# One reader for the third product's bank, and an expert's six scaled additions spread over the next products, in a three-stage attention and mixture-of-experts kernel

## The chip, the cores and the metric

The kernel runs on one core of a Trainium2 chip. The metric is the device time of one execution in microseconds (us): before the change the median of three runs is 1606.64 us (1606.39 to 1607.98). One further execution was recorded by the hardware profiler; its rows are what this document reads.

The engines are called by the profile's names: PE is TensorE's matmul side, PEld its weight load, DVE is VectorE, ACT is ScalarE, POOL is GpSimd, and SP issues the DMAs.

## The reference

Three layers follow each other, on 1536 tokens of width 512, all in float32:

```
attn_out = _attn_ref(q, k, v, proj)         # attention inside hash buckets
x = _moe_ref(x=x, w_in, w_out)              # g = h * tanh(softplus(h)); 512 -> 2048 -> 512
P = exp(x @ w_gate - max); 8 rounds of row and column normalisation
for e in range(8):
    h = np.maximum(x @ w1[e], 0.0)          # 512 -> 1024
    ye = h @ w2[e]                          # 1024 -> 512
    out += P[:, e:e + 1] * ye
```

The change lies in the last loop, for experts 1 to 7 (expert 0 is computed with the middle layer).

## The kernel before

**Precision.** Each float32 operand is split into a rounded high part and the rest; a product is three matmuls (high by high, high by rest, rest by high). So every value that is to be multiplied again needs two instructions: one that writes the rounded part, one that writes the rest.

**Units.** The loop at the end of the file runs over 56 units: two halves of the tokens (768 each), seven experts, four blocks of 256 hidden columns. A unit has two passes. In the first, seven block products (`PRODUCTS`, a Strassen-like scheme with seven products in place of eight) give the four blocks of the hidden matrix, called 11, 22, 21 and 12, each 128 partitions by 384 tokens. In the second (`second`, `second_mm`), 36 matmuls multiply the four blocks, after the ReLU, by a slice of `w2` and add into six PSUM tiles `y`, one for each 128 tokens of the half. The `y` tiles collect over the four units of an expert. Then `gather` (L1199) adds each of the six, scaled by its column of `P`, to the result in `acc`.

**Banks.** The seven products share two PSUM banks, bank 0 and bank 1. A product is six matmuls (L1122, two blocks of the contraction by three parts). Products 0, 2, 4 and 6 go to bank 0, products 1, 3 and 5 to bank 1. Product 4 starts bank 0 anew; products 2, 3, 5 and 6 add to what their bank holds. After each product, `post` reads the bank: after product 0 ACT copies it to `p1` (L1149); after 1, 3, 4, 5 and 6 DVE adds something to it (L1142: `u`, `v`, and the blocks 22, 21 and 12). After product 2 the bank holds block 11 and is read twice: ACT writes its ReLU, rounded (`rounded`, L1130), and DVE copies it (L1155), since L1135 needs the unrounded block later for the rest. A product that writes a bank waits until the bank has been read.

**Order.** Every engine's order is the order of the program text (the scheduler is manual). Each unit also prepares the weights of later units: ACT rounds them (L982, L983, L1000, L1007), POOL forms sums and rests (L987, L988, L994 to L997, L1004, L1011), SP loads the next block after two of these. After every fourth unit the six `gather`s stand in DVE's order directly behind the second pass, before the next unit's `u`:

```
    def settle():
        for d in done:
            gather(*d)
        done.clear()
```

In the last unit, `settle` comes after each matmul instead, so that a tile is added as soon as it is complete.

Of the kernel before, what the change touches and what calls it, by code (L numbers as in the profile page):

```python
# [57 lines left out]
def lsh_attention_moe_kernel(  # L58
# [13 lines left out]
    nc = tc.nc  # L72
# [974 lines left out]
    for i in range(RING_A + NX + 1, NW):  # L1047
        need = free[i - RING] + 1 if i >= RING else 0
        if NATT <= i < N64:
            nd = max(nd, free_dec.get(i - NDEC, 0))  # L1050
            for j in range(2):
                d = int(nd)
# [11 lines left out]
    for n in range(NST + LAG):  # L1064
# [30 lines left out]
        s=wb_p.tile([P, 2, 1024], F32R, name="ws"), a=wb_p.tile([P, 2, 768], F32R, name="wa"),  # L1095
# [17 lines left out]
    bank, val, hid_u, y_t = {}, {}, {}, {}  # L1113

    def product(u, s):
        a, b, x, first = PRODUCTS[s]
        if first:
            bank[x] = ps_u.tile([P, 512], F32, tag=f"u{(u + x) % 2}", name="u")[:, :HALF]
        n = 0
        for kc in range(KC // 2):  # L1120
            for m, mm in ((0, 0), (0, 1), (1, 0)):
                nc.tensor.matmul(bank[x], weight(u, a, m, kc), moving(u, b, mm, kc), start=(first and n == 0), stop=(n == 5), skip_group_check=not first)  # L1122
                n += 1

    def temp(tag, bufs=1):
        return c_p.tile([P, HALF], F32, tag=tag, name=tag, bufs=bufs)

    def rounded(u, c, src):
        hi = h_p.tile([P, HALF], F32R, tag=f"h{c}", name="gh")
        nc.scalar.activation(hi, src, AF.Relu)  # L1130
        hid_u[u, c] = [hi]

    def rest(u, c, src):
        lo = h_p.tile([P, HALF], F32R, tag=f"l{c}", name="gl")
        nc.vector.scalar_tensor_tensor(  # L1135
            out=lo, in0=src, scalar=0.0, in1=f32(hid_u[u, c][0]), op0=ALU.max, op1=ALU.subtract
        )
        hid_u[u, c].append(lo)

    def total(tag, x, y):  # L1140
        t = val[tag] = temp(tag)
        nc.vector.tensor_add(t, x, y)  # L1142
        return t

    def post(u, s):
        a, b = bank[0], bank.get(1)
        if s == 0:
            val["p1"] = temp("p1")
            nc.scalar.copy(val["p1"], a)  # L1149
        elif s == 1:  # L1150
            total("u", b, val["p1"])
        elif s == 2:
            rounded(u, "11", a)
            val["c11"] = temp("c11")
            nc.vector.tensor_copy(val["c11"], a)  # L1155
        elif s == 3:
            total("v", b, val["p1"])
        elif s == 4:
            rounded(u, "22", total("c22", a, val["v"]))
        elif s == 5:  # L1160
            rounded(u, "21", total("c21", b, val["p1"]))
        else:
            rounded(u, "12", total("c12", a, val["u"]))
            for c in ("11", "22", "21", "12"):
                rest(u, c, val["c" + c])

    def second(u):
        tiles = {c: range(3 * int(c[1]) - 3, 3 * int(c[1])) for c in ("11", "22", "21", "12")}
        order = [(c, t, m) for c in ("11", "22") for t in tiles[c] for m in (0, 1)]
        if u == NU - 1:  # L1170
            for c, d in (("11", "21"), ("22", "12")):
                for t in tiles[c]:
                    order += [(c, t, 2)] + [(d, t, m) for m in range(3)]
        else:
            order += [(c, t, 2) for c in ("11", "22") for t in tiles[c]]
            order += [(c, t, m) for c in ("21", "12") for t in tiles[c] for m in (0, 1)]
            order += [(c, t, 2) for c in ("21", "12") for t in tiles[c]]
        return [
            (c, t, m, all(x[1] != t for x in order[:n]), all(x[1] != t for x in order[n + 1:]))
            for n, (c, t, m) in enumerate(order)  # L1180
        ]

    def second_mm(u, c, t, m, first, last):
        g, e, k = unit(u)
        if first and k == 0:
            y_t[t] = ps_z.tile([P, 512], F32, tag=f"z{t}", name="y")
        hi, lo = hid_u[u, c]
        y = wbuf[u % 2]["w"][:, int(m == 1), (int(c[0]) - 1) * 512:int(c[0]) * 512]
        nc.tensor.matmul(  # L1189
            y_t[t], (hi, hi, lo)[m][:, t % 3 * P:(t % 3 + 1) * P], y,  # L1190
            start=(k == 0 and first), stop=(k == NF // 2 - 1 and last),
        )
        if last and k == NF // 2 - 1:
            done.append((g, e, t))

    def gather(g, e, t):
        i = g * 6 + t
        dst = acc[:, i // KC, i % KC, :]
        nc.vector.scalar_tensor_tensor(  # L1199
            out=dst, in0=y_t[t], scalar=prob[:, i, e:e + 1], in1=dst, op0=ALU.mult, op1=ALU.add  # L1200
        )
        if e == E - 1:
            nc.sync.dma_start(out=out[i * P:(i + 1) * P, :], in_=dst)
# [7 lines left out]
    NRUN = 4  # L1211
# [30 lines left out]

    done = []

    def settle():
        for d in done:
            gather(*d)
        done.clear()

    def run_jobs(u, s):  # L1250
        for f in jobs.pop((u, s), []):
            f()

    for u in range(NU):
        run_jobs(u, -1)
        for s in range(NP1):
            product(u, s)
            post(u, s)
            run_jobs(u, s)
        downs = second(u)  # L1260
        for r in range(NRUN):
            for x in downs[len(downs) * r // NRUN:len(downs) * (r + 1) // NRUN]:
                second_mm(u, *x)
                if u == NU - 1:
                    settle()
            settle()
            run_jobs(u, NP1 + r)
    assert not jobs, jobs.keys()

# [49 lines left out]
```

## Time and profile before

| | |
|---|---|
| median of three runs | 1606.64 us |
| the profiled execution | 1608.38 us |
| its span, first to last instruction | 1606.6 us |
| PE busy | 1560.1 us, 97% |
| PEld busy | 1335.7 us, 83% |
| DVE busy | 957.3 us, 60% |
| POOL busy | 875.9 us, 55% |
| ACT busy | 642.4 us, 40% |
| mean granted TensorE clock | 0.999 |

The loop over the 56 units fills the span from about 704 us to its end. How to read the rows: a group of the timeline starts at the time in the first column, lasts as long as the second says, and the brackets at its end give how long the engine had been idle before it and what ended that. "x6" is the number of instructions in the group. In a query for one line, the three durations are the shortest, the median and the longest.

### The profile page before, as it was taken

To read this page: it belongs to the slowest core of one execution; us is meant where nothing else is said; L and a number is where in the kernel's file an instruction comes from. 1 tells how busy PE (TensorE), PEld (TensorE's weight loads), DVE (VectorE), ACT (ScalarE), POOL (GpSimd) and SP (SyncE) were. 2 spreads that over 40 slices of the span, in tenths; PEclk is the share of its full clock that TensorE was granted. 3 is DMA by queue.
4 is the path that set the end of the run, shared out by engine and by line. 5 is a ranking of instruction groups with operands and counts; after the bars stand their busy time and mean duration, and the time that the engine had idled before them with its cause. 6 is when DMAs were issued, how large, how long until landed. Compare 5 with 4: busy or idle time off the path is not lost.

```text
span 1606.6 us, 20403 instructions
## 1 busy us (share of the span) xinstructions
PE 1560.1 (97%) x7407; PEld 1335.7 (83%) x7407; DVE 957.3 (60%) x1536; ACT 642.4 (40%) x1167; POOL 875.9 (55%) x697
## 2 busy tenths in 40 slices
PE   7889999999999999999999999999999999999998
PEld 5777777888888878888888888888888888888887
DVE  7999998687883223666553544767535444445353
ACT  4767766644333322233333333333433333333331
POOL 4787867443333330236666666666666666666661
PEclk9999999999999999999999999999999999999999
DMA  6645442021222010012222222222322222222211
GB/s 144 170 111 132 122 129 72 27 77 54 66 66 79 0 53 1 27 40 66 66 66 66 66 66 66 66 66 66 105 66 66 66 66 66 66 66 66 66 53 40
DMA packets 62644, 113.46 MB, mean 71 GB/s; under 512 B 18176, under 2 KB 18920, under 8 KB 62544
## 3 DMA queue, kind: packets, MB, share of 16 engines
q1 hardware_dynamic: 62544, 112.17, 23.6%
q8 instruction: 58, 0.95, 0.3%
q14 instruction: 42, 0.34, 0.1%
HBM read 89.22 MB, written 3.15 MB: 57 GB/s over the span
## 4 chain that ended last, share of the span: by engine, by line
PE 80%; DVE 14%; ACT 2%; DMA 2%; issue 1%; SPq 0%; POOL 0%; ACTq 0%; DVEq 0%
PE y L1189 27%; PE u L1122 21%; PE y L823 12%; PE h L787 4%; PE h L789 4%; PE h L788 4%; DVE acc L1199 3%; PE pav L487 3%; DVE mx L399 2%; DVE c L1155 2%; ACT gh L1130 1%; PE ps L385 1%; PE pst L437 1%; PE pst L438 1%; DVE bit L343 0%
## 5 line engine op out<-in xcount | busy, mean ns | idle before, releaser
L1142 DVE TENSOR_TENSOR u<-u,p 128x384 f32<-128x384 f32 x56 | 31.1, 555 | 251.6 <-PE u L1122 251.6
L449 POOL TENSOR_TENSOR plo<-p,ph 128x384 fp32r<-128x384 f32 x128 | 142.5, 1124 | 69.1 <-ACT ph L446 37.3
L1130 ACT ACTIVATE gh<-c 128x384 fp32r<-128x384 f32 x168 | 88.3, 525 | 209.3 <-DVE c L1142 209.3
L1135 DVE SCALAR_TENSOR_TENSOR gl<-c,gh 128x384 fp32r<-128x384 f32 x224 | 168.5, 814 | 0.0
L1189 PE MATMUL y<-ww,gh 128*128 128x512 f32 x672 | 163.4, 391 | 0.0
L1189 PE MATMUL y<-w,gh 128*128 128x512 f32 x672 | 162.6, 391 | 0.0
L1189 PEld LDWEIGHTS y<-w,gh 128*128 128x128 f32 x672 | 125.7, 188 | 25.2
L1189 PEld LDWEIGHTS y<-ww,gh 128*128 128x128 f32 x672 | 125.7, 188 | 25.2
L1011 POOL TENSOR_TENSOR w<-stage,w 128x1024 fp32r<-128x1024 f32 x28 | 66.9, 2391 | 83.0 <-ACT w L1007 83.0
L157 POOL TENSOR_TENSOR stage<-stage,sgn 128x512 f32<-128x512 f32 x32 | 46.5, 1453 | 119.9 <-DVE sgn L155 48.3
L823 PE MATMUL y<-gh,w 128*128 128x512 f32 x336 | 110.3, 389 | 0.0
L1004 POOL TENSOR_TENSOR w<-sraw,w 128x1024 fp32r<-128x1024 f32 x28 | 68.5, 2447 | 76.0 <-ACT w L1000 76.0
L443 ACT ACTIVATE p<-pst 128x384 f32<-128x384 f32 x192 | 93.1, 489 | 36.1 <-PE pst L438 30.7
L1011 POOL TENSOR_TENSOR ww<-stage,ww 128x1024 fp32r<-128x1024 f32 x28 | 67.1, 2395 | 72.8 <-ACT ww L1007 72.8
L787 PE MATMUL h<-xh,w 128*128 128x512 f32 x252 | 99.5, 395 | 0.0
L987 POOL TENSOR_TENSOR wa<-stage,wa 128x512 fp32r<-128x512 f32 x28 | 38.5, 1374 | 109.6 <-ACT wa L982 85.8
L399 DVE TENSOR_REDUCE mx<-ps 128x1 f32<-128x768 f32 x95 | 89.9, 946 | 13.9 <-PE ps L385 13.3
L788 PE MATMUL h<-xl,w 128*128 128x512 f32 x252 | 98.2, 390 | 0.0
L789 PE MATMUL h<-xh,w 128*128 128x512 f32 x252 | 98.1, 389 | 0.0
L1122 PE MATMUL u<-tw,w 128*128 128x384 f32 x420 | 85.8, 344 | 8.5 <-DVE u L1142 5.1
L1122 PE MATMUL u<-tw,ws 128*128 128x384 f32 x420 | 88.0, 344 | 4.6 <-DVE c L1155 4.6
L1122 PEld LDWEIGHTS u<-tw,w 128*128 128x128 f32 x420 | 72.5, 188 | 17.5 <-DVE u L1142 9.3
(246 smaller groups left out, 4006.6 us busy)
## 6 DMA issues: line engine op xcount, KB each, us to landing
stage<-in_w_dram SPq DMA_DIRECT2D x152, 512.0 KB
raw<-in_qk_dram SPq DMA_DIRECT2D x13, 384.0 KB
wx<-hi SPq DMA_DIRECT2D x20, 192.0 KB
vt<-in_v_dram SPq DMA_DIRECT2D x16, 192.0 KB
out_dram<-acc SPq DMA_DIRECT2D x12, 256.0 KB
zq<-hi SPq DMA_DIRECT2D x11, 192.0 KB
ak<-hi SPq DMA_DIRECT2D x11, 192.0 KB
zq<-lo SPq DMA_DIRECT2D x11, 192.0 KB
```

Source lines behind the costliest of these rows:

```text
L399: nc.vector.tensor_reduce(out=m[:, t:t + 1], in_=s_t[t][:, :, :HALF], axis=AX.XY, op=ALU.max)
L443: nc.scalar.activation(p_t[u, c], st_t.pop((u, c))[:, :HALF], AF.Exp, scale=0.125)
L449: (nc.gpsimd if e == "P" else nc.vector).tensor_sub(out, in0, in1)
L787: nc.tensor.matmul(t, wt[:, 0, f], xh[:, kc, c], start=(kc == 0), stop=False)
L788: nc.tensor.matmul(t, wt[:, 0, f], xl[:, kc, c], start=False, stop=False)
L789: nc.tensor.matmul(t, wt[:, 1, f], xh[:, kc, c], start=False, stop=(kc == KC - 1))
L823: nc.tensor.matmul(yps[j], x, y, start=(head and m == 0), stop=(tail and m == 2))
L1011: nc.gpsimd.tensor_sub(y[:, 1, :], t, f32(y)[:, 0, :])
L1122: nc.tensor.matmul(bank[x], weight(u, a, m, kc), moving(u, b, mm, kc), start=(first and n == 0), stop=(n == 5), skip_group_check=not first)
L1130: nc.scalar.activation(hi, src, AF.Relu)
L1135: nc.vector.scalar_tensor_tensor(out=lo, in0=src, scalar=0.0, in1=f32(hid_u[u, c][0]), op0=ALU.max, op1=ALU.subtract)
L1189: nc.tensor.matmul(y_t[t], (hi, hi, lo)[m][:, t % 3 * P:(t % 3 + 1) * P], y, start=(k == 0 and first), stop=(k == NF // 2 - 1 and last),)
```

## The change

After product 2, ACT copies the bank into `c11` and rounds from that copy; DVE's copy goes. `settle` takes a number: two of an expert's six additions stay behind the second pass, the other four are written after products 0, 2, 4 and 5 of the next unit.

```diff
         elif s == 2:
-            rounded(u, "11", a)
             val["c11"] = temp("c11")
-            nc.vector.tensor_copy(val["c11"], a)
+            nc.scalar.copy(val["c11"], a)
+            rounded(u, "11", val["c11"])
         elif s == 3:
...
-    def settle():
-        for d in done:
+    def settle(n=None):
+        for d in done[:n]:
             gather(*d)
-        done.clear()
+        del done[:n]
...
             product(u, s)
             post(u, s)
+            settle(s in (0, 2, 4, 5))
             run_jobs(u, s)
...
                 if u == NU - 1:
                     settle()
-            settle()
+            if r == NRUN - 1:
+                settle(2)
             run_jobs(u, NP1 + r)
```

ACT's order in a unit, from the weight rounding that begins it to the first three ReLUs (`p` is `p1`, `u` the bank, `c` the blocks):

```order
 L1007 CAST w_76<-stage 128x1024
 L1149 COPY p_6888<-u 128x384
-L1130 ACTIVATE gh<-u 128x384
+L1154 COPY c_6909<-u 128x384
+L1130 ACTIVATE gh<-c_6909 128x384
 L1130 ACTIVATE gh<-c_6928 128x384
 L1130 ACTIVATE gh<-c_6938 128x384
```

ACT has one instruction more, and the first one behind `p1` is now the copy; the ReLU reads SBUF.

DVE's order in the first unit of an expert, before, from the six additions on:

```order
L1199 SCALAR_TENSOR_TENSOR acc<-y,prob,acc 128x512 x6
L1142 TENSOR_TENSOR u<-u,p_7804 128x384
L1155 COPY c_7827<-u 128x384
L1142 TENSOR_TENSOR v<-u,p_7804 128x384
L1142 TENSOR_TENSOR c_7844<-u,v 128x384
L1142 TENSOR_TENSOR c_7854<-u,p_7804 128x384
L1142 TENSOR_TENSOR c_7864<-u 128x384
L1135 SCALAR_TENSOR_TENSOR gl<-c_7827,gh 128x384
```

And in the changed kernel, the same place:

```order
L1199 SCALAR_TENSOR_TENSOR acc<-y,prob,acc 128x512 x3
L1142 TENSOR_TENSOR u<-u,p_7800 128x384
L1199 SCALAR_TENSOR_TENSOR acc<-y,prob,acc 128x512
L1142 TENSOR_TENSOR v<-u,p_7800 128x384
L1142 TENSOR_TENSOR c_7842<-u,v 128x384
L1199 SCALAR_TENSOR_TENSOR acc<-y,prob,acc 128x512
L1142 TENSOR_TENSOR c_7853<-u,p_7800 128x384
L1199 SCALAR_TENSOR_TENSOR acc<-y,prob,acc 128x512
L1142 TENSOR_TENSOR c_7864<-u 128x384
L1135 SCALAR_TENSOR_TENSOR gl<-c_7822,gh 128x384
```

Three additions now stand before `u` (two behind the second pass, one after product 0), the fourth before `v`, the fifth between the blocks 22 and 21, the sixth between 21 and 12; the copy of the bank is gone. In the other units DVE's order is the same but for the missing copy.

## Rows read from the trace of the kernel before

**Rows 1.** The page: busy us (share of the span) x instructions of each engine.
```profile
PE 1560.1 (97%) x7407; PEld 1335.7 (83%) x7407; DVE 957.3 (60%) x1536; ACT 642.4 (40%) x1167; POOL 875.9 (55%) x697
```

**Rows 2.** Waits of PEld from 700 us on: total us, times, longest.
```profile
PEld u L1122 <- DVE c L1155: 21.9, 43, 1.4
PEld u L1122 <- DVE u L1142: 9.3, 13, 1.5
```

**Rows 3.** Timeline, an ordinary unit's products: start, us, engine, line, operation [idle before].
```profile
1251.85 0.48 ACT L1149 COPY p<-u 128x384 f32<-128x384 f32 x1
...
1252.91 0.56 DVE L1142 TENSOR_TENSOR u<-u,p 128x384 f32<-128x384 f32 x1 [6.84 <-PE u L1122]
...
1253.52 1.07 PEld L1122 LDWEIGHTS u<-tw,w 128*128 128x128 f32 x6
...
1253.93 0.49 ACT L1130 ACTIVATE gh<-u 128x384 fp32r<-128x384 f32 x1 [1.60 <-PE u L1122]
...
1254.45 0.56 DVE L1155 COPY c<-u 128x384 f32<-128x384 f32 x1 [0.99 <-ACT gh L1130]
1254.95 0.56 DVE L1142 TENSOR_TENSOR v<-u,p 128x384 f32<-128x384 f32 x1
...
1255.07 1.01 PEld L1122 LDWEIGHTS u<-tw,w 128*128 128x128 f32 x6 [0.48 <-DVE c L1155]
...
1256.06 1.06 PEld L1122 LDWEIGHTS u<-tw,wx 128*128 128x128 f32 x6
```

**Rows 4.** Timeline, the first unit of an expert.
```profile
1281.57 4.05 DVE L1199 SCALAR_TENSOR_TENSOR acc<-y,prob,acc 128x512 f32<-128x512 f32 x6 [3.54 <-PE y L1189]
...
1285.53 0.55 DVE L1142 TENSOR_TENSOR u<-u,p 128x384 f32<-128x384 f32 x1
...
1286.14 2.06 PEld L1122 LDWEIGHTS u<-tw,w 128*128 128x128 f32 x12 [0.64 <-DVE u L1142]
...
1287.51 0.56 DVE L1142 TENSOR_TENSOR v<-u,p 128x384 f32<-128x384 f32 x1 [0.53 <-PE u L1122]
...
1288.18 1.05 PEld L1122 LDWEIGHTS u<-tw,wx 128*128 128x128 f32 x6
...
1288.55 0.56 DVE L1142 TENSOR_TENSOR c<-u,v 128x384 f32<-128x384 f32 x1 [0.48 <-PE u L1122]
...
1289.59 0.56 DVE L1142 TENSOR_TENSOR c<-u,p 128x384 f32<-128x384 f32 x1 [0.48 <-PE u L1122]
...
1290.43 2.92 PE L1189 MATMUL y<-w,gh 128*128 128x512 f32 x12
1290.63 0.56 DVE L1142 TENSOR_TENSOR c<-u 128x384 f32<-128x384 f32 x1 [0.48 <-PE u L1122]
1291.11 3.06 DVE L1135 SCALAR_TENSOR_TENSOR gl<-c,gh 128x384 fp32r<-128x384 f32 x4
...
1292.40 1.35 POOL L987 TENSOR_TENSOR wx<-stage,wx 128x512 fp32r<-128x512 f32 x1 [3.26 <-ACT wx L982]
```

**Rows 5.** Timeline, the very first unit, and PEld in the first unit after four.
```profile
708.63 0.48 ACT L1130 ACTIVATE gh<-u 128x384 fp32r<-128x384 f32 x1
...
709.76 1.00 PEld L1122 LDWEIGHTS u<-tw,w 128*128 128x128 f32 x6 [1.45 <-DVE c L1155]
...
773.66 2.06 PEld L1122 LDWEIGHTS u<-tw,w 128*128 128x128 f32 x12 [1.53 <-DVE u L1142]
```

**Rows 6.** Queries by line: duration ns min/median/max, first and last start.
```profile
L1149 ACT COPY p<-u x56: 481/481/483, 705.5 to 1588.1; 128x384 f32<-128x384 f32 x56
...
L1155 DVE COPY c<-u x56: 542/558/559, 709.2 to 1590.7; 128x384 f32<-128x384 f32 x56
...
L1135 DVE SCALAR_TENSOR_TENSOR gl<-c,gh x224: 546/552/1657, 713.7 to 1596.6; 128x384 fp32r<-128x384 f32 x112
```

**Rows 7.** One unit's stretch: us, busy (x) by engine, PEclk, DMA share, GB/s.
```profile
1256.00:1272.00 16.00, 15.84 (x80) 14.07 (x79) 6.25 (x10) 5.37 (x9) 9.93 (x9) 1.00 0.20 66
```

**Rows 8.** Line L1007 on ACT: its engine sat idle before it (us, times) until.
```profile
  PE y L1189: 278.5, 54
```

## The prediction

> **What bounds the kernel now.** The first view is the page's busy table: PE is busy for 97% of the span [rows 1], so only its idle time and what delays its matmuls can be won. A share of 97% hides small stalls, because a matmul that waits overlaps the one before it; the weight loads in front of the matmuls (PEld, 83%) show them better. So the second view is the list of waits of PEld, from the start of the 56 units on. It has two rows and no others: 43 waits for DVE's copy in L1155, 21.9 us, and 13 for DVE's `u` in L1142, 9.3 us [rows 2]. 43 + 13 = 56: one stall in each unit, 31.2 us in all.
>
> The third view is the timeline, for the place of each. In an ordinary unit ACT's ReLU of block 11 reads bank 0 at 1253.93, DVE's copy of the same bank starts at 1254.45, behind it, and ends at 1255.01; product 4, which writes bank 0 anew, starts its loads at 1255.07 after 0.48 us idle [rows 3]. In the first unit of an expert the six additions hold DVE from 1281.57 to 1285.62, `u` ends at 1286.08, and product 3, which adds to the bank that `u` reads, starts at 1286.14 after 0.64 us idle [rows 4]. The stall there is earlier, so that product 4 finds its bank free.
>
> That an idle stretch of PEld is lost time is seen by comparing starts. From product 3 to product 5 it is 1256.06 - 1253.52 = 2.54 us where product 4 stalls [rows 3], and 1288.18 - 1286.14 = 2.04 us where it doesn't [rows 4]: 0.50 against the 0.48 shown. One product is thus 1.02 us. PE's granted clock in such a stretch is 1.00, its upper level (2.4 GHz), with the stalls in it [rows 7].
>
> **The copy.** What goes is one DVE copy per unit (0.558 us, L1155 [rows 6]) and the wait of product 4 for it. What comes is one ACT copy per unit; the nearest row is ACT's copy of the same shape from the same kind of bank, L1149, 0.481 us [rows 6]. From product 3's first load at time 0 the times in an ordinary unit are [rows 3, 4, 6]:
> - ACT starts at 1253.93 - 1253.52 = 0.41, as its ReLU did. The copy ends at 0.41 + 0.48 = 0.89. From the reader's end to PE's load the rows show 0.06 (1255.01 to 1255.07; 1286.08 to 1286.14), so the bank is free at 0.95. Product 4 is due at 1.02. It doesn't wait, with 0.07 to spare. The upper bound for the copy's duration is the DVE copy, 0.558: free at 1.03, a stall of 0.01. The lower is 0.48, no stall. I take 0.48, the same operation on the same engine.
> - `v` is next. It reads bank 1 after product 3, and product 5 waits for it. In the first unit of an expert, where DVE had nothing before it, it started 1287.51 - 1286.14 = 1.37 after product 3's first load, so it ends at 1.93, free at 1.99; product 5 is due at 2.04. No wait, 0.05 to spare. Should `v` start only at 1254.95 - 1253.52 = 1.43, where it does now behind the copy, it would be free at 2.05, a stall of 0.01.
> - Block 22 (product 4 to product 6) has the same distance as `v` and didn't stall in either unit.
>
> The other edge of the step: the ReLU now stands behind the copy on ACT and reads SBUF. Nothing on ACT is due before block 22's ReLU, a product later, and the rounded block 11 is needed by the second pass, more than 2 us later. ACT is busy for 5.37 of 16 us [rows 7], and 0.5 us more is hidden in that idle time. DVE's rest of block 11 (L1135) needs `c11` only after block 12. So the stall of an ordinary unit goes, with nothing in its place.
>
> The very first unit is an exception: its stall is 1.45 us, since ACT had other roundings before its ReLU at 708.63 [rows 5]. The copy there ends at 708.63 + 0.48 = 709.11, PE may go at 709.17 instead of 709.76: 0.59 won, 0.86 kept.
>
> **The additions.** An addition takes 4.05 / 6 = 0.68 us in sequence [rows 4]. Two stay behind the second pass, the third follows after product 0, and they begin at 1281.57 as before and end near 1283.6. `u` can't begin before product 1 ends; PE reaches product 3's load at 1286.14 - 0.64 = 1285.50 if it isn't held, and in the ordinary unit `u` starts 1253.52 - 1252.91 = 0.61 before that load. So `u` is free to start at 1284.89, over 1 us after the third addition, and the 0.64 us go. Of the unit after the first expert, 1.53 us [rows 5], the 0.89 us above the others is the scaling (L903) that stands between its additions and `u`; it fits into that 1 us too.
>
> The fourth addition stands between `u` and `v`: from 1285.45 to 1286.13, and `v` is due at 1285.50 + 1.37 = 1286.87. The fifth stands between block 22, which ends at 1288.55 - 0.64 + 0.56 = 1288.47, and block 21, due at 1289.59 - 0.64 = 1288.95. It ends at 1289.15, so block 21 is 0.2 us late. Block 21 then lasts to 1289.71, the sixth addition to 1290.39, and block 12, due at 1290.63 - 0.64 = 1289.99, is 0.4 us late. Who waits for these? No product of this unit: product 6 adds to bank 0, which block 22 has left. The second pass, which begins at 1290.43 - 0.64 = 1289.79, takes 2.92 us for twelve matmuls and only then needs the rest of block 11, at 1292.7 (0.24 us a matmul). That rest now starts 1291.11 - 1290.63 = 0.48 after block 12 did, at 1290.87, and is done 0.55 later [rows 6], at 1291.42: more than 1 us to spare. The new waits are those of the second pass for the fifth and sixth `y` tiles: its ninth and eleventh matmul, at 1289.79 + 8 x 0.24 = 1291.7 and 1292.2, need additions that end at 1289.15 and 1290.39. Both are covered.
>
> One rule speaks against this part. The last row of the additions' unit shows four rests taking 3.06 us [rows 4] where the median of one is 0.552 and the longest 1.657 [rows 6]; the long one lies beside POOL's L987, which begins at 1292.40 [rows 4]. The Trainium skill (SBUF — State Buffer, Who interferes with whom) states that a VectorE instruction with two SBUF inputs and a GpSimd one that reads SBUF lock each other out for a whole instruction; the additions, with one input from PSUM, would be exempt, the rests not. By that rule, rests pushed 0.4 us later are caught sooner, and where PE needs the one that is caught the time is that of the second rival below, not the sum; the trace agrees that a rest can be caught (1.657 us).
>
> **The sum.** 31.2 us of stalls [rows 2] less the 0.86 that the first unit keeps: 30.3 us. The span becomes 1606.6 - 30.3 = 1576.3. The profiled execution was 1608.38 us, 1.8 above its span, and the median of the runs 1606.64, 1.7 below that execution; the gain taken off the median gives 1606.64 - 30.3 = 1576.3 us. From a unit of 16 us this is half a microsecond, 3%.
>
> **Rivals.**
> - A small wait stays in every unit (chance 0.07). The margins above are 0.05 to 0.07 us, and bounds missed by 0.01. If copy and `v` were 0.1 us later than their nearest rows, 56 x 0.1 = 5.6 us stay: 1582. For it: the smallness of the margins. Against: `u` after product 1 has the same distance and no stall in an ordinary unit [rows 3].
> - The spread additions cost what they won (0.06): block 12's delay pushes DVE's rests into POOL's L987, one that PE needs is held for 1.66 - 0.55 = 1.1 us, and 0.6 of it shows. 13 x 0.64 = 8.3 us come back: 1584.6. Against: L987 waits for ACT's rounding, which stands behind block 12's ReLU, so that it moves with the rests.
> - Something else sets the unit's length, and nothing is won (0.02): 1606. Against: in 16 us POOL is busy for 9.93, DVE 6.25, ACT 5.37, the DMA engines at 0.20 [rows 7].
> - Slower (0.05): product 4 now waits for ACT, whose order has the rounding L1007 and `p1` before the copy. If units that come 0.5 us sooner made L1007 wait for its weights from memory, all three would be late. ACT's 1.60 us of idle time before its read [rows 3] has to be used up first, and from another 0.6 us on (copy's end after 1255.01) the stall is larger than now. At 1 us of stall in place of 0.48 in the 56 units the time is 1606.6 + 56 x 0.5 = 1635. Against: L1007 waited for PE only, 54 times, never for a DMA [rows 8].
>
> **How the numbers follow.** The full gain has 0.80. Its own range is 1574.5 (the sum with the first unit's stall gone as well, and a little of the run-to-run spread) to 1579 (0.05 us of stall left in each unit). The range for 8 in 10 adds the first two rivals: 1574.5 to 1586. A change of 0.2% (3.2 us) is about what a measurement of this kernel can tell from none. Faster by more than that: 0.80 + 0.07 + 0.06 = 0.93; within it 0.02; slower 0.05.
>
> **What would show it.** In the changed profile PEld has one wait worth naming after 700 us, the first unit's of about 0.9 us; the starts of products 3, 4 and 5 are 1.02 to 1.04 apart in every unit, also in the first of an expert; product 4's releaser, where one is named, is ACT's copy; that copy lasts 0.48 us and starts 0.41 after product 3's load; `v` starts about 0.06 earlier against product 3; and the granted clock stays at 1.00. A row of PEld waits for ACT with 0.1 us or more per unit would make the first rival right, one of L1189 for DVE the second, and idle time of ACT before L1007 put down to a DMA the last.

## The result, and the profile after

The changed kernel takes 1580.78 us (median of four runs, 1580.21 to 1581.5) against 1606.52 for the kernel before: a ratio of 0.9838, 95% interval 0.9821 to 0.9855. Timed once more beside more runs of the kernel before, it is 1580.19 against 1607.54, ratio 0.983 (0.9817 to 0.9844). The profiled execution took 1580.8 us.

The list of waits of PEld from 695 us on, which had 31.2 us in 56 waits [rows 2], in the changed kernel (total us, times, longest):

```profile
PEld u L1122 <- ACT c L1154: 0.9, 1, 0.9
PEld u L1122 <- DVE u L1142: 0.3, 1, 0.3
```

Two waits are left of 56; the second, of `u`, stands in a unit that had none of this kind before (last section). The timeline of an ordinary unit's products, to be read beside [rows 3]:

```profile
1235.52 0.56 DVE L1142 TENSOR_TENSOR u<-u,p 128x384 f32<-128x384 f32 x1 [6.84 <-PE u L1122]
...
1236.13 2.11 PEld L1122 LDWEIGHTS u<-tw,w 128*128 128x128 f32 x12
...
1236.49 0.48 ACT L1154 COPY c<-u 128x384 f32<-128x384 f32 x1 [1.60 <-PE u L1122]
...
1237.00 0.53 ACT L1130 ACTIVATE gh<-c 128x384 fp32r<-128x384 f32 x1
1237.56 0.56 DVE L1142 TENSOR_TENSOR v<-u,p 128x384 f32<-128x384 f32 x1 [1.48 <-PE u L1122]
...
1238.23 1.05 PEld L1122 LDWEIGHTS u<-tw,wx 128*128 128x128 f32 x6
```

Products 3 and 4 are now one group of twelve loads with no gap. ACT's copy ends at 1236.97, 0.84 us after product 3's first load, and the ReLU follows it from SBUF. Products 3 and 5 start 2.10 us apart, where it was 2.54.

The first unit of an expert, beside [rows 4]; DVE's rows first, then the loads:

```profile
1263.28 2.07 DVE L1199 SCALAR_TENSOR_TENSOR acc<-y,prob,acc 128x512 f32<-128x512 f32 x3 [3.54 <-PE y L1189]
1266.59 0.56 DVE L1142 TENSOR_TENSOR u<-u,p 128x384 f32<-128x384 f32 x1 [1.24 <-PE u L1122]
1267.06 0.74 DVE L1199 SCALAR_TENSOR_TENSOR acc<-y,prob,acc 128x512 f32<-128x512 f32 x1
1268.62 0.56 DVE L1142 TENSOR_TENSOR v<-u,p 128x384 f32<-128x384 f32 x1 [0.82 <-PE u L1122]
1269.66 0.56 DVE L1142 TENSOR_TENSOR c<-u,v 128x384 f32<-128x384 f32 x1 [0.48 <-PE u L1122]
1270.14 0.74 DVE L1199 SCALAR_TENSOR_TENSOR acc<-y,prob,acc 128x512 f32<-128x512 f32 x1
1270.80 0.55 DVE L1142 TENSOR_TENSOR c<-u,p 128x384 f32<-128x384 f32 x1
1271.26 0.74 DVE L1199 SCALAR_TENSOR_TENSOR acc<-y,prob,acc 128x512 f32<-128x512 f32 x1
1271.92 0.55 DVE L1142 TENSOR_TENSOR c<-u 128x384 f32<-128x384 f32 x1
```
```profile
1267.20 2.11 PEld L1122 LDWEIGHTS u<-tw,w 128*128 128x128 f32 x12
...
1269.29 1.05 PEld L1122 LDWEIGHTS u<-tw,wx 128*128 128x128 f32 x6
```

After three additions DVE waits for PE (1.24 us before `u`), not PE for DVE. The fifth and sixth addition make the blocks 21 and 12 start 1.14 and 1.12 us after the one before, in place of 1.04; no load waits for them.

The chain of waits that ended last shows the units as PE alone (start, us, engine, line):

```profile
1217.78 7.33 PE u L1122 x42
1225.11 8.20 PE y L1189 x36
```

A unit is 7.33 + 8.20 = 15.53 us. Before, it was 15.98 in an ordinary unit (product 4 of neighbouring units started at 1255.07 [rows 3] and 1271.05, below; the mean of all of them is 15.975), and 16.12 in the first unit of an expert, by the chain's second passes there:

```profile
1274.47 7.08 PE y L1189 x31
...
1290.59 8.20 PE y L1189 x36
```

The stretch of the 56 units is the part that the change touches. It runs from the first load of the first unit to the first matmul of the last second pass. Before:

```profile
704.04 0.19 PEld L1122 LDWEIGHTS u<-xh,wx 128*128 128x128 f32 x1
...
1271.05 1.01 PEld L1122 LDWEIGHTS u<-tw,ws 128*128 128x128 f32 x6 [0.48 <-DVE c L1155]
...
1594.51 2.92 PE L1189 MATMUL y<-ww,gh 128*128 128x512 f32 x12
```

After:

```profile
703.73 0.19 PEld L1122 LDWEIGHTS u<-xh,wx 128*128 128x128 f32 x1
...
1566.68 2.92 PE L1189 MATMUL y<-ww,gh 128*128 128x512 f32 x12
```

890.47 us against 862.95: 27.5 us are won in the units.

### The profile page after: what moved, and what is told of

Its sections match the earlier page's. It is cut to its first block, busy times and chain, and to the rows that moved or that the text cites. A ratio compares the mean times of both kernels' runs of the same rounds, so it can differ in the third digit from the quotient of the medians.

```text
span 1578.8 us, 20184 instructions
## 1 busy us (share of the span) xinstructions
PE 1544.8 (98%) x7407; PEld 1337.7 (85%) x7407; DVE 925.7 (59%) x1480; ACT 671.2 (43%) x1223; POOL 879.4 (56%) x697
## 4 chain that ended last, share of the span: by engine, by line
PE 87%; DVE 9%; DMA 1%; ACT 1%; issue 1%; SPq 0%; DVEq 0%; ACTq 0%
PE y L1189 29%; PE u L1122 26%; PE y L823 12%; PE h L787 4%; PE h L789 4%; PE h L788 4%; PE pav L487 3%; DVE mx L399 3%; PE ps L385 1%; PE pst L437 1%; PE pst L438 1%; DVE xu L516 0%; DVE col L404 0%; DVE bit L343 0%; DVE sgn L135 0%
## 5 line engine op out<-in xcount | busy, mean ns | idle before, releaser
L1142 DVE TENSOR_TENSOR u<-u,p 128x384 f32<-128x384 f32 x56 | 31.2, 558 | 267.1 <-PE u L1122 267.1
L1130 ACT ACTIVATE gh<-c 128x384 fp32r<-128x384 f32 x224 | 117.9, 526 | 154.4 <-DVE c L1142 152.7
L449 POOL TENSOR_TENSOR plo<-p,ph 128x384 fp32r<-128x384 f32 x128 | 142.7, 1125 | 68.6 <-ACT ph L446 36.5
L399 DVE TENSOR_REDUCE mx<-ps 128x1 f32<-128x768 f32 x95 | 89.8, 946 | 13.5 <-PE ps L385 12.9
L1007 ACT CAST ww<-stage 128x1024 fp32r<-128x1024 f32 x28 | 29.5, 1052 | 141.0 <-PE y L1189 141.0
L1007 ACT CAST w<-stage 128x1024 fp32r<-128x1024 f32 x28 | 29.4, 1050 | 137.6 <-PE y L1189 137.6
L1189 PE MATMUL y<-ww,gl 128*128 128x512 f32 x336 | 86.1, 389 | 0.0
```

Of the source, the lines that this page charges most:

```text
L399: nc.vector.tensor_reduce(out=m[:, t:t + 1], in_=s_t[t][:, :, :HALF], axis=AX.XY, op=ALU.max)
L449: (nc.gpsimd if e == "P" else nc.vector).tensor_sub(out, in0, in1)
L1189: nc.tensor.matmul(y_t[t], (hi, hi, lo)[m][:, t % 3 * P:(t % 3 + 1) * P], y, start=(k == 0 and first), stop=(k == NF // 2 - 1 and last),)
```

## The experiments

Each kernel was also compared with the kernel before on the same chip; a ratio is to that one.

**One part alone: the copy.** The changed `post`, with the old `settle`:

```diff
     def settle():
         for d in done:
             gather(*d)
         done.clear()
...
-            rounded(u, "11", a)
             val["c11"] = temp("c11")
-            nc.vector.tensor_copy(val["c11"], a)
+            nc.scalar.copy(val["c11"], a)
+            rounded(u, "11", val["c11"])
```

> Only the copy and the rounding from it are changed; the six additions stay behind the second pass, as before. Theory (each stall is its own term, sized by the start-to-start loss of 0.45 us, not by the 0.48 us of idle weight load): the 42 ordinary stalls and 0.59 us of the first go, the 13 waits of product 3 for u stay: 42 x 0.45 + 0.6 = 19.5 us, 1587 us. Rival (every unit gains by the copy, the first units of an expert too): 25 us, 1581 us. Prediction's own size (idle of the weight load): 42 x 0.485 + 0.6 = 21 us, 1585.5 us.

Measured: 1588.04 us against 1608.0, ratio 0.9878 (0.9865 to 0.9892), about 20 us. The waits of PEld:

```profile
PEld u L1122 <- DVE u L1142: 9.6, 14, 1.5
PEld u L1122 <- ACT c L1154: 0.9, 1, 0.9
```

The ordinary stalls are gone and the 13 for `u` stand as before, with one of 0.3 us that the changed kernel has too. The rival of 25 us is out. The intervals are too wide to tell 19.5 from 21, but the stretch of the units tells them apart:

```profile
701.57 0.19 PEld L1122 LDWEIGHTS u<-xh,wx 128*128 128x128 f32 x1
...
1573.15 2.70 PE L1189 MATMUL y<-ww,gh 128*128 128x512 f32 x11
```

871.58 us against 890.47 before: 18.9 us are won. Less the new wait of 0.3 us, the theory's 19.5 makes 19.2 and the prediction's own 21 makes 20.7; two profiles of one kernel agree in this stretch to about 0.1 us (below), so the latter is out.

**The other part alone: the additions.** The new `settle` with the old `post`:

```diff
-            val["c11"] = temp("c11")
-            nc.scalar.copy(val["c11"], a)
-            rounded(u, "11", val["c11"])
+            rounded(u, "11", a)
+            val["c11"] = temp("c11")
+            nc.vector.tensor_copy(val["c11"], a)
```

> Only the additions are spread; DVE still copies bank 0 behind ACT's ReLU. Theory (the parts are not additive): the first units of an expert lose their wait for u, but product 4 then waits for DVE's copy as in an ordinary unit (0.45 us), and the fourth addition, between copy and v, makes v late for product 5 by about 0.2 to 0.3 us; so 13 x 0.6 is won and about 13 x 0.7 lost: 1606 us, within 2 us. Rival (the spread is worth its 13 x 0.64 us by itself): 1598 us.

Measured: 1606.08 us against 1608.0, ratio 0.999 (0.9981 to 0.9999). PEld waits once in each unit, all for the copy:

```profile
PEld u L1122 <- DVE c L1155: 28.7, 56, 1.5
```

In the first unit of an expert (DVE and PEld, from the copy on):

```profile
1284.45 0.56 DVE L1155 COPY c<-u 128x384 f32<-128x384 f32 x1 [0.99 <-ACT gh L1130]
1284.92 0.74 DVE L1199 SCALAR_TENSOR_TENSOR acc<-y,prob,acc 128x512 f32<-128x512 f32 x1
1285.06 1.00 PEld L1122 LDWEIGHTS u<-tw,w 128*128 128x128 f32 x6 [0.50 <-DVE c L1155]
...
1285.58 0.55 DVE L1142 TENSOR_TENSOR v<-u,p 128x384 f32<-128x384 f32 x1
...
1286.18 1.00 PEld L1122 LDWEIGHTS u<-tw,wx 128*128 128x128 f32 x6
```

The stall for `u` has turned into that for the copy, one product later. The fourth addition then makes `v` late: product 5 starts 1.12 us after product 4, where after a stall it was 0.99 [rows 3]; the pause before it, 0.12 us, is too short for the list of waits. The stretch of the units:

```profile
703.72 0.19 PEld L1122 LDWEIGHTS u<-xh,wx 128*128 128x128 f32 x1
...
1592.16 2.01 PE L1189 MATMUL y<-ww,gh 128*128 128x512 f32 x8
```

888.44 us, 2.0 less than before. By the times the spread gives at most 3 us by itself, and the rival's 8 us are out. The two parts alone win 18.9 and 2.0 us in the units, both together 27.5: 6.6 us come only when both waits are gone.

**The read made longer.** The changed kernel with ACT's copy made twice:

```diff
             nc.scalar.copy(val["c11"], a)
+            nc.scalar.copy(val["c11"], a)
             rounded(u, "11", val["c11"])
```

> The changed kernel with ACT's copy of bank 0 made twice, one behind the other, into the same tile. Theory (what PE waits for is the end of the last read of the bank): free at about 0.41 + 2 x 0.48 + 0.06 = 1.43 us after product 3's first load, due at 1.05, so 0.3 to 0.4 us of stall in each of 56 units comes back, put down to L1154 (or its doubled line) on ACT: 1598 to 1602 us. Rival (product 4 would have been held by something else anyway, the margin is large): 1581 us.

Measured: 1597.72 us against 1608.0, ratio 0.9938 (0.9925 to 0.9952). The waits of PEld, and a unit:

```profile
PEld u L1122 <- ACT c L1155: 20.0, 55, 1.4
PEld u L1122 <- DVE u L1142: 0.3, 1, 0.3
```
```profile
1246.21 1.05 PEld L1122 LDWEIGHTS u<-tw,w 128*128 128x128 f32 x6
...
1246.57 0.48 ACT L1154 COPY c<-u 128x384 f32<-128x384 f32 x1 [1.60 <-PE u L1122]
1247.08 0.48 ACT L1155 COPY c<-u 128x384 f32<-128x384 f32 x1
...
1247.61 1.00 PEld L1122 LDWEIGHTS u<-tw,w 128*128 128x128 f32 x6 [0.35 <-ACT c L1155]
```

A second copy, which ends 0.51 us after the first, brings back 0.35 us of wait in the unit shown (55 waits in all), put down to that copy: PE waits for the end of the bank's last read. 0.16 of the 0.51 us were covered: that is the changed kernel's margin.

**The kernel before, profiled again.** No edit.

> The kernel before, unchanged, profiled a second time. Theory (the first profiled execution lay 1.8 us above the median, and that is in the attention stage, ahead of the 56 units): the units take the same to 0.3 us as in the first profile, and if the time is near 1606.5 the part before 700 us is shorter by about 1.8 us. Rival (the units themselves vary): the units' stretch is shorter by 1.8 us.

Measured: 1607.99 us, so this execution wasn't one near 1606.5. Its first load of the units:

```profile
703.78 0.19 PEld L1122 LDWEIGHTS u<-xh,wx 128*128 128x128 f32 x1
...
1594.13 0.86 PE L1189 MATMUL y<-ww,gh 128*128 128x512 f32 x3
```

The units take 890.35 us, against 890.47 in the first profile: they agree, and the rival is out. For what lies ahead of the units this run is inconclusive; the next one speaks for it.

**The changed kernel again.** No edit.

> The changed kernel, unchanged, timed again beside more runs of the kernel before. Theory (27 us are won in the 56 units: 42 x 0.455 + 13 x 0.595 + 0.6, and what lies ahead of them varies by about 2 us from run to run): 27 us less than the kernel before, ratio 0.983. Rival (the first comparison of medians, 25.7 us, is the true size and 1.5 us of it are lost elsewhere): ratio 0.984 and a later start of the 56 units in the profile.

Measured: 1580.19 us against 1607.54, ratio 0.983 (0.9817 to 0.9844), 27.3 us. Its first load of the units:

```profile
701.85 0.19 PEld L1122 LDWEIGHTS u<-xh,wx 128*128 128x128 f32 x1
```

That is 1.88 us earlier than in the first profile of the same program, and its span is 2.0 us shorter (1576.8 against 1578.8). The units themselves take 862.82 us (their last second pass begins at 1564.67), against 862.95 in the first profile. So what lies ahead of the units varies by about 2 us between executions (where is shown in the last section), and the rival's later start didn't come. The 25.7 us of the first medians fit 27.5 less that scatter; where runs without a profile spent their time isn't shown.

**The other reader.** The changed kernel with DVE making the one read:

```diff
-            nc.scalar.copy(val["c11"], a)
+            nc.vector.tensor_copy(val["c11"], a)
             rounded(u, "11", val["c11"])
```

> The changed kernel with the one read of bank 0 made by DVE in place of ACT; ACT still rounds from the copy. Theory (the gain is from one reader in place of two in series, whoever it is): free at 0.41 + 0.56 + 0.06 = 1.03 us after product 3's first load, due at 1.05: no stall, or under 0.03 us a unit; within 1.5 us of the changed kernel. Rival (it is ACT's shorter copy, or DVE's queue being free for v, that does it): 0.1 us or more in each unit, 6 us or more slower than the changed kernel.

Measured: 1578.27 us, ratio 0.9818 (0.9805 to 0.9832), beside the changed kernel's 1580.19. PEld waits for nothing in the 56 units, the first included. A unit:

```profile
1232.87 2.09 PEld L1122 LDWEIGHTS u<-tw,w 128*128 128x128 f32 x12
...
1233.24 0.56 DVE L1154 COPY c<-u 128x384 f32<-128x384 f32 x1 [0.42 <-PE u L1122]
1233.89 0.53 ACT L1130 ACTIVATE gh<-c 128x384 fp32r<-128x384 f32 x1 [2.20 <-DVE c L1154]
1234.28 0.56 DVE L1142 TENSOR_TENSOR v<-u,p 128x384 f32<-128x384 f32 x1 [0.48 <-PE u L1122]
...
1234.95 1.05 PEld L1122 LDWEIGHTS u<-tw,wx 128*128 128x128 f32 x6
```

So the gain is that of one reader in place of two in series, whichever it is. The 1.2 us of waits that the changed kernel keeps are gone here: the 0.9 us of the first unit because DVE has none of that unit's roundings in its order, the 0.3 us of the late `u` for a reason that no run shows. The units take 861.89 us (701.49 to 1563.38), about 1 us less than in the changed kernel's two profiles. The times agree in sign, but their intervals overlap, so that they don't resolve this difference.

**No reads between the products.** All readings of the two banks stand behind product 6:

```diff
     def post(u, s):
         a, b = bank[0], bank.get(1)
+        if s != 6:
+            return
...
```

> All reads of both banks are put behind product 6, so that products 2 to 6 wait for no reader (the blocks are then not the right sums; this leaves out the readings in between). The whole is slower, since the second pass waits for all of them. What is looked at is the pitch of the seven products: theory (1.045 us a product is the floor of 42 such matmuls, and nothing of the margins of 0.05 us is paid) 7.3 us from the first product's load to the second pass's place, products 3 to 5 2.09 apart; rival (about 0.04 us of hidden wait a product is left in the changed kernel) 7.1 us or less, products 3 to 5 2.04 apart.

Measured: 1674.87 us in one run. The loads of products 3, 4 and 5:

```profile
1240.48 2.10 PEld L1122 LDWEIGHTS u<-tw,ws 128*128 128x128 f32 x12
1242.56 1.05 PEld L1122 LDWEIGHTS u<-tw,wa 128*128 128x128 f32 x6
```

2.08 us without any reader to wait for, against 2.10 and 2.09 in the changed kernel; the chain gives 7.32 us for the 42 matmuls against 7.33. The changed kernel's products are at this floor to 0.02 us in two products; the rival's 0.04 us a product isn't there.

## Why the prediction was right, and where its size was off

The mechanism came as forecast, the time 4.5 us above the forecast and inside the range.

- *The copy.* The stalls of ordinary units went with nothing in their place: `copy_only` shows it alone. The copy lasted 0.48 us, the ReLU behind it cost PE nothing, and `v` came in time. Its margin was put at 0.07 us and is 0.16 (`copy_twice`): product 4 is due at 1.05 and not at 1.02, and the copy starts 0.36 us after product 3's first load, not 0.41. `v` didn't come earlier, as one of the signs had it: it still starts 1.43 us after that load, since the 1.37 was read behind a stall. That is in time because product 5 is due at 2.10, not at 2.04.
- *The very first unit.* It was to keep 0.86 us of its 1.45; PEld's wait there is 0.9, put down to L1154, as forecast.
- *The additions.* `u` is free, PE doesn't wait for the fifth and sixth `y` tile or for a rest. The delays of block 21 and 12 were put at 0.2 and 0.4 us; they are 0.10 and 0.18: in the rows above DVE starts an instruction 0.08 to 0.09 us before the end of the one ahead. The first units of an expert gain only together with the copy, which `spread_only` shows; the prediction had counted them in one sum without saying so.
- *The sum.* This is the term that was mis-sized: 31.2 us of idle weight load was taken for lost time. The prediction checked it against the distance of products 3 and 5 in the first unit of an expert, 2.04 us, and made one product 1.02 us. But those two products follow a stall, after which six loads take 1.01 us in place of 1.07 [rows 3]: part of the idle time is made up. Without a stall the distance is 2.09 to 2.10 (`no_reads_between`: 2.08), a product 1.04 to 1.05, and an ordinary stall costs 15.98 - 15.53 = 0.45 us in the unit shown, 0.44 on average, not 0.48 to 0.50; one of `u` 16.12 - 15.53 = 0.59, not 0.64. The sum is 42 x 0.44 + 13 x 0.59 + 0.6 = 26.8 us, and the extra 0.9 of the unit after the first expert less 0.3 for the late `u` below makes 27.4; the stretch of the units shows 27.5. `copy_twice` over-reads in the same way: its waits are 19.1 us more than the changed kernel's (20.0 + 0.3 less 1.2), its units only 16.8 us longer (703.65 to 1583.37).
- *The base.* The remaining 1.8 us are between 27.5 and the first medians' 25.7. With more runs the difference is 27.3, so they are most likely scatter ahead of the units.
- *The rivals.* No small wait stays in every unit, the rests are not caught where PE needs them (the fourth of a unit takes 1.65 us in both kernels, and no matmul waits for it), nothing else sets the unit's length, and ACT's read is late in the first unit alone: L1007 still waits for PE only (278.5 us, 54 times), never for a DMA.

## What to carry to other kernels

Where a PSUM bank is read by two engines one behind the other and then written again, let one engine read it and the rest work from its copy: the writer waits for the last reader. Two waits on one path hide each other, so their removal is worth more together (27.5 us of the units) than the sum of each alone (20.9). And size a stall from the starts of the work on either side of it, in a place that doesn't follow another stall, not from the idle time shown in front of the loads.

## What the runs showed of the hardware that was not expected

An idle stretch of PEld reads about 0.045 us longer than what it costs here: 0.48 us shown and 0.44 lost, 0.64 and 0.59, and in `copy_twice` 19.1 and 16.8 us over 55 stalls.

In one unit of the changed kernel, the 19th, `u` starts 0.35 us late with DVE idle for 7.20 us and nothing ahead of it (PEld's wait at 987.68, and at 985.76 in the second profile of the same program). `copy_only` and `copy_twice` have it in the same unit; with DVE reading the bank it is absent. So it goes with the program and not with one execution; its cause stays open.

The 2 us ahead of the units can be placed. Up to 21.8 us the two profiles of the changed kernel run alike, PE busy without a gap from 19 us on. Then, in the attention layer, the second one's granted clock goes from 0.50 (20 to 21 us, the lower level of 1.2 GHz) to 1.00 (22 to 23 us, 2.4 GHz), PE's matmuls come faster, and DVE's maximum of their result (L399) starts at 23.41 in place of 24.09. So DVE's next instruction, L404, and POOL's L449 come in another order. In the first profile:

```profile
24.80 1.80 POOL L449 TENSOR_TENSOR lo<-rs,hi 128x768 fp32r<-128x768 f32 x1
25.08 1.54 DVE L404 TENSOR_SCALAR col<-mx 128x3 f32<-128x3 f32 x1
```

In the second:

```profile
24.40 0.41 DVE L404 TENSOR_SCALAR col<-mx 128x3 f32<-128x3 f32 x1
24.74 1.81 POOL L449 TENSOR_TENSOR lo<-rs,hi 128x768 fp32r<-128x768 f32 x1
```

The same small instruction takes 1.54 us where it starts 0.28 us behind POOL's, and ends 0.02 us after it; it takes 0.41 us where it starts first. 0.68 us earlier and 1.13 us shorter make 1.8 of the 1.9 us. `copy_only` also starts its units early (701.57) although its L404 took 1.54 us, so there are other sources of this scatter.
